# First projection of eight block pairs by seven half-size products

## The chip, the cores and the metric

The kernel runs on one core of a Trainium2 chip. The metric is the time of one execution on the device, in microseconds (us). The kernel before took 327.92 us (median of three runs, 327.44 to 328.18).

A core has five engines, each with its own queue of instructions that it works through in order: TensorE (PE; its weight loads are shown as PEld), VectorE (DVE), ScalarE (ACT), GpSimd (POOL) and SyncE (SP, which here only starts transfers). They wait for each other by semaphores. TensorE's products land in PSUM, which has eight banks of 128 partitions x 512 f32 values; VectorE and ScalarE read them from there.

## The reference

Sparse attention of 8 batches x 8 heads x 576 tokens x 64 values (four heads with a local mask, four with a strided one) gives x, 4608 tokens x 512. Then comes a bilinear feed-forward layer with d_ff = 1536:

```python
a = x @ w_a          # 4608 x 512 times 512 x 1536
b = x @ w_b
out = (a * b) @ w_out
```

The change touches only `a`, for some tokens and some features.

## The kernel before

**Tiles.** The 4608 tokens are nine tiles of 512 (`TTOK`, t = 0 to 8, `NT` = 9). x is held transposed in `xT`: 128 partitions x `KD` = 4 slices of the inner dimension x a ring of four batches of tokens. The 1536 features are `FD` = 12 blocks of 128. Two neighbouring blocks, 2g and 2g + 1, are pair g.

**First projection** (`ffn_ab`, `ab_mm`). For each tile and block, a takes four products of 128x128 weights with 512 tokens, one for each slice of the inner dimension, summed in one PSUM bank; b takes four more in another. ScalarE copies a to `a_sb` (L638), VectorE multiplies it by b from PSUM into `pf` (bf16, L641), in an order of tokens that suits the second projection.

**Second projection.** Tiles 2 to 8 (`FAST_Y`) take it by seven products instead of eight on halves of the tokens, of the inner dimension and of the output columns (`products`, `y_plan`, and `y_tail` for the last tile). It needs sums of parts of `pf` (`fast_s`, L655, on VectorE, into `ps`) and of the weights (`fast_w`, L174, once). In the last tile, `y_tail` uses narrow banks that each take several results in turn: ScalarE copies one out (L686) and the next group of products goes into the same bank.

**Banks.** From the second stage on PSUM is cut into `mm` (three banks, in turn), `tp` (one bank), `o` (two banks) and `st` (two banks). `mm_bank` hands out mm, mm, mm, tp in a cycle of four. `st` and `o` belong to the attention, which runs one batch ahead of the feed-forward tiles; its last steps (batch 7) lie in tile 6. A bank is handed on only when whoever reads it is done.

**Order.** The program is written in the order in which each engine gets its instructions (a manual schedule). The main loop runs over slots, 16 to a tile: twelve blocks of the first projection, four quarters of the second. After each slot it issues what is tied to it: attention steps (`take`), and the list `at` (loads, transposes, `fast_s`). Where a slot has such a list, GpSimd first copies one value of the slot's result to `pace` (L947), so that what it issues next does not come too early.

Of the kernel before, what the change touches and what calls it, by code (L numbers as in the profile page):

```python
# [7 lines left out]
F32 = mybir.dt.float32  # L8
BF16 = mybir.dt.bfloat16
I16 = mybir.dt.int16  # L10
ALU = mybir.AluOpType
# [13 lines left out]
VW = 128  # L25
WCH = (0, 2, 5, 9, 12)
FAST_Y = (2, 3, 4, 5, 6, 7, 8)


@with_exitstack  # L30
def kernel(
# [10 lines left out]
    nc = tc.nc  # L42
    B, H, S, D = q.shape
# [5 lines left out]
    KD = d_model // 128  # L49
    FD = d_ff // 128  # L50
    TTOK = 512
    NT = n_tok // TTOK
# [7 lines left out]
    fsb = ctx.enter_context(tc.tile_pool(name="ffn", bufs=2))  # L60
    pst = ctx.enter_context(tc.tile_pool(name="pst", bufs=1, space=bass.MemoryType.PSUM))
    dram = ctx.enter_context(tc.tile_pool(name="dram", bufs=2, space=bass.MemoryType.DRAM))

    psum4 = {}

    def open_psum(stack, **bufs):
        for nm, n in bufs.items():
# [8 lines left out]
    qz_pair = [(const.tile([128, 2, 2, S], BF16, name=f"qz{i}l"), const.tile([128, 2, 2, RS * GP], BF16, name=f"qz{i}s"))  # L76
               for i in range(2)]
    qz_buf = [[tuple(t[:, j] for t in pair) for j in range(2)] for pair in qz_pair]
    kT_buf = [(const.tile([128, 2, PAD + S], BF16, name=f"kT{i}l"), const.tile([128, 2, RS * GP + 48], BF16, name=f"kT{i}s"))
              for i in range(2)]  # L80
    vl_buf = [const.tile([128, HL * 6, VW], BF16, name=f"vl{i}") for i in range(2)]
# [76 lines left out]
    XR = 4  # L158
    xT = const.tile([128, KD, XR * S], BF16)
    wa_sb = wp.tile([128, KD, d_ff], BF16)  # L160
    wb_sb = wp.tile([128, KD, d_ff], BF16)
    wo_sb = wp.tile([128, FD, d_model], BF16)

    FG = FD // 2
    HT = TTOK // 2
# [437 lines left out]
    pfs = {}  # L603
# [3 lines left out]
    def mm_bank(shape):  # L607
        nm = "tp" if used[0] % 4 == 3 and used[0] >= 0 else "mm"
        used[0] += 1
        return psum4[nm].tile(shape, F32, tag=nm, name="mm")  # L610

    def ab_mm(t, f, ab, kks, mid=None, first=0, last=KD - 1, ws=(0, 1)):
        n = min(TTOK, XR * S - TTOK * t % (XR * S))
        cuts = [(0, n)] + ([(n, TTOK - n)] if n < TTOK else [])
        for w, ps_ in [((wa_sb, wb_sb)[i], ab[i]) for i in ws]:
            if mid and ps_ is ab[1]:
                mid()
            for kk in kks:
                for c0, n in cuts:
                    x0 = (TTOK * t + c0) % (XR * S)  # L620
                    nc.tensor.matmul(ps_[:, c0:c0 + n], lhsT=w[:, kk, 128 * f:128 * (f + 1)], rhs=xT[:, kk, x0:x0 + n],  # L621
                                     start=(kk == first and c0 == 0), stop=(kk == last and c0 == cuts[-1][0]))

    def ffn_ab(t, f, mid, ab=None):
        if f == 0:
            pfs[t] = fsb.tile([128, FD, TTOK], BF16, tag="pf", name="pf", bufs=1)
        pf = pfs[t]
        if ab is None:
            ab = [mm_bank([128, TTOK]) for _ in range(2)]
            if f == 0:  # L630

                late = 1 if t == 1 else 3
                ab_mm(t, f, ab, [kk for kk in range(KD) if kk != late], last=-1)
                ab_mm(t, f, ab, [late], first=-1, last=late)
            else:
                ab_mm(t, f, ab, range(KD), mid)
        a_sb = fsb.tile([128, TTOK], F32, tag="a_sb", name="a_sb")
        nc.scalar.copy(a_sb, ab[0])  # L638
        if t in FAST_Y:
            halves = lambda x: x.rearrange("p (a i s) -> p a i s", i=2, s=16)  # L640
            nc.vector.tensor_mul(pf[:, f, :].rearrange("p (i a s) -> p a i s", i=2, s=16), halves(a_sb), halves(ab[1]))  # L641
        else:
            nc.vector.tensor_mul(pf[:, f, :], a_sb, ab[1])  # L643
        return pf[:1, f, :1]

    pss = {}

    def fast_s(t, n, gs):
        if t not in pss:
            pss[t] = nat.tile([128, FG * 5 * SW], BF16, tag="shared", name="ps").rearrange("p (n g m) -> p n g m", g=FG, n=5)  # L650
        s = pss[t][:, :, gs, :HT]
        x = pfs[t].rearrange("p (g e) (i m) -> p e i g m", e=2, i=2)[:, :, :, gs]
        a, b, op = ((x[:, 0, 1], x[:, 1, 1], ALU.add), (s[:, 0], x[:, 0, 0], ALU.subtract),
                    (x[:, 0, 0], x[:, 0, 1], ALU.subtract), (x[:, 1, 0], s[:, 1], ALU.subtract))[n]
        nc.vector.tensor_tensor(s[:, n], a, b, op=op)  # L655

    yst = {}
# [144 lines left out]
    with tc.manual_schedule(engines={ENG.PE, ENG.SP, ENG.Pool, ENG.DVE, ENG.Activation}):  # L802
# [30 lines left out]
        for nm in ORDER:  # L833
            if nm[0] == "*":
                spin(int(nm[1:]))
            elif nm == "C0":
                for x, cp, n in ((raw[0], nc.vector.tensor_copy, "k"), (raw[1], nc.scalar.copy, "q")):
                    t = nats[0, n, False][:, 0:2].rearrange("p h r d -> p (h r d)")
# [21 lines left out]
            elif nm[0] == "F":  # L860
                f = int(nm[1])
# [6 lines left out]
                elif nm == "F0B":  # L868
                    first[f].append(psum4["o"].tile([128, 512], F32, tag="o", name="ab"))
                ab_mm(0, f, first[f], {"A": (0, 1), "B": (0, 1), "b": (2,), "c": (3,)}[nm[2]],  # L870
                      ws={"A": (0,), "B": (1,)}.get(nm[2], (0, 1)))
# [5 lines left out]
        for t in range(NT):  # L877
            slots += [(ffn_ab, t, f) for f in range(FD)] + [(ffn_ys if t in FAST_Y else ffn_y, t, j) for j in range(4)]
        for b in range(1, B):
# [9 lines left out]
        def do(i, fn, *args):  # L889
            at.setdefault(i, []).append(lambda: fn(*args))  # L890

        soon = {}
        for t in FAST_Y[:-1]:
            soon[16 * t + 10] = [lambda t=t: fast_s(t, 2, slice(4, 6))]
            soon[16 * t + 11] = [lambda t=t, n=n: fast_s(t, n, slice(4, 6)) for n in (0, 1)]
# [5 lines left out]
        for b in range(FIRST_D, B):  # L901
            g0 = 16 * (b - 2)
            if b == FIRST_D:
                do(0, load_qk, b, False)
                do(1, load_qk, b, True)
                do(16, load_vl, b)
                for h in range(HL):
                    do(20 + h, load_vs, b, (h,))
            else:
                for h in range(HL):  # L910
                    do(g0 + h + (2 if b == FIRST_D + 1 else -2), load_qk, b, False, (h,))
                    do(g0 + h + (6 if b == FIRST_D + 1 else 2), load_qk, b, True, (h,))
                    do(g0 + h + 10, load_vs, b, (h,))
                do(g0 + (10 if b == FIRST_D + 1 else 7), load_vl, b)
            gs = {2: (14, 14, 15, 15, 16, 16, 17, 17, 18, 18), 3: (8, 9, 10, 11, 12, 13, 14, 15, 16, 17)}.get(b) or (
                3, 5, 7, 9, 12, 13, 14, 15, 16, 17)
            for (z, nm, part), g in zip(((0, "k", 0), (0, "k", 1), (0, "q", 0), (0, "q", 1), (1, "k", 0), (1, "k", 1),
                                         (1, "k", 2), (1, "q", 0), (1, "q", 1), (1, "q", 2)), gs):
                if (b, z, nm, part) != (FIRST_D, 0, "k", 1):
                    do(g0 + g, step_D, b, z, nm, part)  # L920
        for h in range(HL):
            do((7, 7, 8, 9)[h], spread_vs, 1, h, nc.vector.tensor_copy)
        do(1, zero_qz, 1, nc.vector, ((1, 1),))
# [7 lines left out]
        for g in range(FG):  # L931
            for n in (2, 0, 1, 3):
                do(16 * (NT - 1) + 2 * g + 1, fast_s, NT - 1, n, slice(g, g + 1))
        for t in FAST_Y[:-1]:
            for slot, n, z0, z1 in ((4, 0, 0, 2), (5, 2, 0, 2), (6, 1, 0, 2), (7, 3, 0, 2), (8, 2, 2, 4), (9, 0, 2, 4),
# [45 lines left out]
```

## Time and profile before

| what | us |
| --- | --- |
| median of three runs | 327.92 |
| the profiled execution | 327.27 |
| its span, first to last instruction | 325.6 |
| first projection of tile 6 (with attention between) | 229.5 to 251.2 |
| first projection of tile 7 | 261.2 to 281.9 |
| first projection of tile 8 | 291.1 to 311.8 |
| second projection of tile 8, products | 311.8 to 321.2 |

The granted TensorE clock is 1.00 throughout. How to read the rows: a group's row has the line, engine, operation, output <- inputs with their shapes, the count, the busy time in us and the mean duration of one in ns, and then the time that the engine sat idle just before them with what ended it. A timeline row has start, length, engine, line and operation; an `xN` row is N such instructions in a row, in square brackets is the idle time before it. A chain row has start, length, and the engine and line of that piece. Matmuls are pipelined: one row lasts longer (379 ns for 512 columns, 273 for 256) than the step from one to the next, which is what a stream of them costs.

### The profile page before, as it was taken

How to read it: one execution, taken by the hardware profiler on the slowest of the kernel's cores; microseconds unless marked ns; L12 is line 12 of the kernel's file. 1: busy time of each engine (PE TensorE's matmuls, PEld its weight loads, DVE VectorE, ACT ScalarE, POOL GpSimd, SP SyncE). 2: the span in 40 equal slices, each digit the busy share in tenths (PEclk: the TensorE clock that was granted, in tenths of full speed). 3: DMA queues.
4: the chain of work that ended last, by engine and by line, in shares of the span. 5: the costliest groups of instructions: out<-in, count | busy, mean ns of one | idle time of the engine just before them, and what ended most of it. 6: DMA issues, size and time to landing. Idle time of an engine off the chain costs nothing.

```text
span 325.6 us, 7280 instructions
## 1 busy us (share of the span) xinstructions
PE 319.7 (98%) x2632; PEld 204.6 (63%) x2632; DVE 247.9 (76%) x530; ACT 183.6 (56%) x305; POOL 150.3 (46%) x279
## 2 busy tenths in 40 slices
PE   8999999999999999999999999999999999999994
PEld 7754565455555587557999885569555944674474
DVE  6766887888778899898889888988877645726652
ACT  6764775478764576457644765476547733323341
POOL 8936739599857554854476247633001001100000
PEclk9999999999999999999999999999999999999999
DMA  9999999899999989999999999899155040004004
GB/s 157 159 204 200 204 182 186 153 176 132 143 210 137 140 86 98 120 215 135 105 98 204 156 97 113 181 193 103 30 128 125 2 129 0 3 0 131 0 0 131
DMA packets 110723, 40.43 MB, mean 124 GB/s; under 512 B 88672, under 2 KB 107744, under 8 KB 110688
## 3 DMA queue, kind: packets, MB, share of 16 engines
q0 software_dynamic: 85968, 19.48, 65.5%
q1 hardware_dynamic: 24576, 20.42, 24.9%
q8 instruction: 21, 0.34, 0.5%
q14 instruction: 14, 0.11, 0.1%
q10 hardware_dynamic: 144, 0.07, 0.1%
HBM read 39.51 MB, written 10.91 MB: 155 GB/s over the span
## 4 chain that ended last, share of the span: by engine, by line
PE 94%; DMA 2%; DVE 1%; ACT 1%; issue 1%; POOL 0%; POOLq 0%
PE mm L621 54%; PE mm L709 17%; PE mm L773 6%; PE st L387 4%; PE o L465 2%; PE o L524 2%; DMA shared<-in_q_dram 2%; PE mm L738 2%; PE end L738 1%; PE ab L621 1%; PE misc L154 1%; PE tp L549 1%; PE tp L295 1%; PE st L400 0%; PE tp L286 0%
## 5 line engine op out<-in xcount | busy, mean ns | idle before, releaser
L621 PE MATMUL mm<-xT,wa_sb 128*128 128x512 bf16 (+1 forms) x472 | 110.3, 357 | 0.0
L621 PE MATMUL mm<-xT,wb_sb 128*128 128x512 bf16 (+1 forms) x472 | 110.2, 357 | 0.0
L638 ACT COPY a_sb<-mm 128x512 f32<-128x512 f32 x106 | 62.1, 586 | 71.3 <-PE mm L621 70.6
L641 DVE TENSOR_TENSOR pf<-a_sb,mm 128x512 bf16<-128x512 f32 x84 | 57.3, 682 | 26.6 <-PE mm L621 22.5
L947 POOL CAST pace<-pf 1x1 f32<-1x1 bf16 x87 | 23.7, 273 | 109.6 <-DVE pf L641 93.1
L621 PEld LDWEIGHTS <-wb_sb 128*128 128x128 bf16 x480 | 46.5, 98 | 44.0 <-issue 0.2
L621 PEld LDWEIGHTS <-wa_sb 128*128 128x128 bf16 x480 | 43.7, 98 | 31.3
L408 ACT ACTIVATE p<-st 72x576 bf16<-72x576 f32 (+1 forms) x56 | 36.4, 650 | 14.7 <-PE st L387 14.5
L540 DVE TENSOR_TENSOR xT<-o,xr 64x288 bf16<-64x288 f32 x48 | 21.4, 446 | 15.3 <-ACT xr L534 14.9
L709 PEld LDWEIGHTS <-ps 128*128 128x128 bf16 x288 | 28.0, 98 | 3.1
L686 ACT COPY y_sb<-mm 128x512 f32<-128x512 f32 (+1 forms) x28 | 15.6, 556 | 17.8 <-PE mm L709 14.5
L709 PE MATMUL mm<-wf,ps 128*128 128x256 bf16 x216 | 25.5, 273 | 0.0
L533 ACT ACTIVATE xr<-o 64x576 f32<-64x576 f32 x28 | 18.1, 648 | 11.9 <-PE o L524 11.6
L773 PE MATMUL mm<-wo_sb,pf 128*128 128x512 bf16 x96 | 23.4, 379 | 0.0
L242 POOL DMA_DIRECT2D vs<-in_v_dram x24 | 19.6, 820 | 4.9 <-PE mm L709 2.4
L709 PEld LDWEIGHTS <-pf 128*128 128x128 bf16 x216 | 20.2, 98 | 2.6 <-issue 0.2
L534 ACT ACTIVATE xr<-xr 64x576 f32<-64x576 f32 x28 | 19.1, 683 | 0.9
L709 PE MATMUL mm<-wo_sb,pf 128*128 128x256 bf16 x144 | 18.5, 273 | 0.1
L211 POOL DMA_DIRECT2D kl<-in_k_dram x24 | 16.0, 667 | 5.5 <-issue 2.9
L211 POOL DMA_DIRECT2D ql<-in_q_dram x24 | 16.2, 674 | 5.0 <-DMA wo_sb<-in_moe_w_out_dram 3.9
L643 DVE TENSOR_TENSOR pf<-a_sb,mm 128x512 bf16<-128x512 f32 x22 | 14.9, 675 | 4.5 <-ACT a_sb L638 3.0
L655 DVE TENSOR_TENSOR ps<-pf 128x512 bf16<-128x512 bf16 (+1 forms) x48 | 17.7, 379 | 0.4
(147 smaller groups left out, 452.9 us busy)
## 6 DMA issues: line engine op xcount, KB each, us to landing
out_dram<-y_sb SPq DMA_DIRECT2D x12, 512.0 KB, 4.8
out_dram<-y_sb SPq DMA_DIRECT2D x11, 256.0 KB, 3.1
vl<-in_v_dram POOLq DMA_DIRECT2D x6, 384.0 KB, 7.7
kl<-in_k_dram POOLq DMA_DIRECT2D x24, 72.0 KB, 3.1
ql<-in_q_dram POOLq DMA_DIRECT2D x24, 72.0 KB, 3.1
vs<-in_v_dram POOLq DMA_DIRECT2D x24, 72.0 KB, 4.2
wo_sb<-in_moe_w_out_dram POOLq DMA_DIRECT2D x4, 384.0 KB, 9.9
natk<-in_k_dram POOLq DMA_DIRECT2D x20, 72.0 KB, 3.4
```

Source lines behind the costliest of these rows:

```text
L211: nc.gpsimd.dma_start(out=t[32 * h:32 * h + 32], in_=src[b, h].rearrange("(i y) d -> y i d", y=32))
L242: nc.gpsimd.dma_start(out=vs_buf[b % 2][:, h, :, 0:D], in_=v[b, HL + h].rearrange("(p r) d -> p r d", r=RS))
L408: nc.scalar.activation(p_flat(p)[:M, :2 * W].rearrange("p (i n) -> p i n", n=2 * n), st[:M].rearrange("p a (i n) -> p (a i) n", n=256)[:, ...
L533: nc.scalar.activation(r, sums, ACT.Ln)
L534: nc.scalar.activation(r, r, ACT.Exp, scale=-1.0)
L540: nc.vector.tensor_mul(dst.rearrange("d (p r) -> d p r", r=RS)[:, :, G * half:G * (half + 1)], o[:64, j, :W].rearrange("d (g p) -> d p g", ...
L621: nc.tensor.matmul(ps_[:, c0:c0 + n], lhsT=w[:, kk, 128 * f:128 * (f + 1)], rhs=xT[:, kk, x0:x0 + n], start=(kk == first and c0 == 0), sto ...
L638: nc.scalar.copy(a_sb, ab[0])
L641: nc.vector.tensor_mul(pf[:, f, :].rearrange("p (i a s) -> p a i s", i=2, s=16), halves(a_sb), halves(ab[1]))
L709: nc.tensor.matmul(bank[b][:, q], lhsT=lhs(g, q), rhs=rhs(g), start=k in "172" and q == 0 and g == 0, stop=g == FG - 1, skip_group_check=True)
L773: nc.tensor.matmul(ybank[j], lhsT=pf[:, f, 128 * j:128 * (j + 1)], rhs=wo_sb[:, f], start=(f == 0), stop=(f == FD - 1))
L947: nc.gpsimd.tensor_copy(pace, done)
```

## The change

Eight pairs, g = 1 to 4 of tile 7 and g = 0 to 3 of tile 8 (`FAST_A`), take `a` of both blocks by seven products instead of eight. The 512 tokens are two halves (k), the inner dimension two halves of two slices each (j), the pair two blocks (e). Each product is two narrow matmuls of 256 columns (c = 0, 1). They need four sums of weight quarters, made once by VectorE in tile 6, and four sums of token quarters per tile. The sums are stored in tiles of the attention that are no longer used (`vl`, `qz`), as are the results of odd pairs (`kT`).

Products 1, 6, 5 and 3 add up in one bank X, in `st` for even g and in `o` for odd g. After each of them ScalarE copies the bank out, as one quarter of the result. Products 7 and 4 share a bank Z, product 2 has Y, and b of the two blocks takes one bank each; these four come from `mm` and `tp`. Product 7 goes by ScalarE to `p7`. VectorE adds Y to quarter (0,0) and Z to quarter (1,0); GpSimd adds `p7` to quarter (1,1). Then VectorE multiplies both blocks, block 2g + 1 first. The matmuls of b are put between the products of a. A pair takes two slots; the first ends behind product 2.

In tile 8, one of the four sums for the second projection (n = 2) of pairs 0 to 2 goes to GpSimd, one pair later. The diff, in its core:

```diff
+FAST_A = {7: (1, 2, 3, 4), 8: (0, 1, 2, 3)}
...
         pf = pfs[t]
+        if f // 2 in FAST_A.get(t, ()):
+            if f % 2 == 0:
+                pairs[t, f // 2] = a_pair(t, f // 2)
+            return next(pairs[t, f // 2])
...
+    wav = wa_sb.rearrange("p (j c) (g e m) -> p j c g e m", c=2, e=2, m=128)
+    wsum_a = [flat.rearrange("p (c g m) -> p c g m", c=2, g=FG)
+              for flat in [vl_buf[0].rearrange("p a b -> p (a b)")[:, 12 * 128 * z:12 * 128 * (z + 1)] for z in range(2)]
+              + [t.rearrange("p a b c -> p (a b c)")[:, :12 * 128] for t in qz_pair[0]]]
+    xsum = {t: qz_pair[1][t - 7].rearrange("p a b c -> p (a b c)")[:, :8 * HT].rearrange("p (n c m) -> p n c m", n=4, c=2)
+            for t in FAST_A}
+
+    def wsum_make(n):
+        w, s_ = (lambda e, j: wav[:, j, :, :, e]), wsum_a
+        a, b, op = ((w(1, 0), w(1, 1), ALU.add), (s_[0], w(0, 0), ALU.subtract), (w(0, 0), w(1, 0), ALU.subtract),
+                    (w(0, 1), s_[1], ALU.subtract))[n]
+        for c in range(2):
+            nc.vector.tensor_tensor(s_[n][:, c], a[:, c], b[:, c], op=op)
+
+    def x_part(t, j, k):
+        x0 = TTOK * t % (XR * S) + HT * k
+        return xT[:, 2 * j:2 * j + 2, x0:x0 + HT]
+
+    def xsum_make(t, n):
+        s_ = xsum[t]
+        a, b = ((x_part(t, 0, 1), x_part(t, 0, 0)), (x_part(t, 1, 1), s_[:, 0]), (x_part(t, 1, 1), x_part(t, 0, 1)),
+                (x_part(t, 1, 0), s_[:, 1]))[n]
+        nc.vector.tensor_tensor(s_[:, n], a, b, op=ALU.subtract)
...
+    def a_pair(t, g):
+        pf = pfs[t]
+        pool, nm = ((pst, "st"), (psum4["o"], "o"))[g % 2]
+        X = pool.tile([128, 2, 512], F32, tag=nm, name="ax")[:, 0, :HT]
+        a = ([fsb.tile([128, TTOK], F32, tag="a_sb", name="a_sb") for _ in range(2)] if g % 2 == 0 else
+             [t.rearrange("p h n -> p (h n)")[:, :2 * TTOK].bitcast(F32) for t in kT_buf[0]])
+        got = {k: psum4[nm].tile([128, TTOK], F32, tag=nm, name="mm")
+               for k, nm in zip((1, "Z", "Y", 0), (("mm", "mm", "tp", "mm"), ("tp", "mm", "mm", "mm"))[g % 2])}
+        Z, Y = got["Z"][:, :HT], got["Y"][:, :HT]
...
+        plan = {"1": (X, w(0, 0), x(0, 0)), "2": (Y, w(0, 1), x(1, 0)), "3": (X, ws(3), x(1, 1)), "4": (Z, w(1, 1), xs(3)),
+                "5": (X, ws(0), xs(0)), "6": (X, ws(1), xs(1)), "7": (Z, ws(2), xs(2))}
...
+        P("1")
+        nc.scalar.copy(quarter(0, 0), X)
+        b_mm(1, (0, 1, 2))
+        P("6")
+        nc.scalar.copy(quarter(1, 0), X)
+        b_mm(1, (3,))
+        P("7")
+        nc.scalar.copy(p7, Z)
+        P("2")
+        nc.vector.tensor_tensor(quarter(0, 0), Y, quarter(0, 0), op=ALU.add)
+        yield None
+        P("5")
+        nc.scalar.copy(quarter(1, 1), X)
+        nc.gpsimd.tensor_tensor(quarter(1, 1), quarter(1, 1), p7, op=ALU.add)
+        if (t, g - 1) in later:
+            later.pop((t, g - 1))()
+        b_mm(0, (0, 1))
+        P("4")
+        nc.vector.tensor_tensor(quarter(1, 0), Z, quarter(1, 0), op=ALU.add)
+        P("3")
+        nc.scalar.copy(quarter(0, 1), X)
+        b_mm(0, (2, 3))
+        mult(1)
+        mult(0)
+        yield pf[:1, 2 * g + 1, :1]
...
+        if (t, n) == (NT - 1, 2) and {gs.start, gs.start + 1} <= set(FAST_A[t]):
+            later[t, gs.start] = lambda: nc.gpsimd.tensor_tensor(s[:, n], a, b, op=op)
+            return
         nc.vector.tensor_tensor(s[:, n], a, b, op=op)
...
+        for n in range(4):
+            do(16 * (NT - 3) + 2 * n + 2, wsum_make, n)
+        do(16 * (NT - 2) - 1, xsum_make, NT - 2, 0)
+        for n in (2, 1, 3):
+            do(16 * (NT - 2), xsum_make, NT - 2, n)
+        for n in range(4):
+            do(16 * (NT - 2) + 12 + n, xsum_make, NT - 1, n)
```

Here `P(k)` issues the two matmuls of product k, `b_mm(e, kks)` those of b of block e for the slices kks, `mult(e)` the multiply of block e, and `quarter(e, k)` is the half k of block e's result.

More of the change, by code (lines that the diff above doesn't have):

```diff
@@ new lines, with P, b_mm, mult @@
+    pairs = {}
+    def a_pair(t, g):
[7 more added lines that the diff above has]
+        Z, Y = got["Z"][:, :HT], got["Y"][:, :HT]
+        p7 = fsb.tile([128, HT], F32, tag="p7", name="p7")
+        quarter = lambda e, k: a[e][:, HT * k:HT * (k + 1)]
+        w = lambda e, j: (lambda c: wav[:, j, c, g, e])
+        ws = lambda n: (lambda c: wsum_a[n][:, c, g])
+        x = lambda j, k: (lambda c: x_part(t, j, k)[:, c])
+        xs = lambda n: (lambda c: xsum[t][:, n, c])
+        plan = {"1": (X, w(0, 0), x(0, 0)), "2": (Y, w(0, 1), x(1, 0)), "3": (X, ws(3), x(1, 1)), "4": (Z, w(1, 1), xs(3)),
+                "5": (X, ws(0), xs(0)), "6": (X, ws(1), xs(1)), "7": (Z, ws(2), xs(2))}
+        def P(k):
+            bank, lhs, rhs = plan[k]
+            for c in range(2):
+                nc.tensor.matmul(bank, lhsT=lhs(c), rhs=rhs(c), start=k in "172" and c == 0, stop=c == 1, skip_group_check=True)
+        x0 = TTOK * t % (XR * S)
+        def b_mm(e, kks):
+            f = 2 * g + e
+            for kk in kks:
+                nc.tensor.matmul(got[e], lhsT=wb_sb[:, kk, 128 * f:128 * (f + 1)], rhs=xT[:, kk, x0:x0 + TTOK],
+                                 start=kk == 0, stop=kk == KD - 1)
+        def mult(e):
+            halves = lambda v_: v_.rearrange("p (a i s) -> p a i s", i=2, s=16)
+            nc.vector.tensor_mul(pf[:, 2 * g + e, :].rearrange("p (i a s) -> p a i s", i=2, s=16),
+                                 halves(a[e]), halves(got[e]))
+        P("1")
[23 more added lines that the diff above has]
+        yield pf[:1, 2 * g + 1, :1]
@@ L646 @@
+    later = {}
     pss = {}
```

## The prediction

> **What bounds the kernel now.** First the page's head and the table of who waited for whom, cut to TensorE:
>
> ```profile
> span 325.6 us, 7280 instructions
> PE 319.7 (98%) x2632; PEld 204.6 (63%) x2632; DVE 247.9 (76%) x530; ACT 183.6 (56%) x305; POOL 150.3 (46%) x279
> ...
> PE misc L154 <- PEq L965: 0.9, 1, 0.9
> PE o L465 <- DVE xr L491: 0.2, 1, 0.2
> PE tp L289 <- DMA shared<-in_q_dram: 0.2, 1, 0.2
> ```
>
> TensorE waits 1.3 us in all, and none of it in the last tiles. So the time is what TensorE has to stream, and a change pays what it takes off that stream minus the gaps that it opens. The chain that ended last, in order of time, prices the stream (start, length, what):
>
> ```profile
> 261.34 20.72 PE mm L621 x96
> 282.06 9.17 PE mm L709 x84
> 291.23 20.72 PE mm L621 x96
> ```
>
> The two L621 rows are the projections of tiles 7 and 8: 20.72 / 96 = 215.8 ns for a product of 512 columns. The L709 row gives 9.17 / 84 = 109.2 ns for one of 256, though its weights change each time. Switching between narrow and wide costs nothing there: the three rows touch.
>
> **What is taken off.** A pair of blocks takes 16 wide products now (8 for a, 8 for b). After, a takes 7 products x 2 halves of the inner dimension = 14 narrow ones, and b keeps 8 wide: 16 x 215.8 = 3453 ns against 14 x 109.2 + 8 x 215.8 = 3255 ns. That is 198 ns a pair and **1.58 us for eight pairs**. All of it lies on TensorE's stream.
>
> **What is added, and beside what.** Prices, from the groups by shape and from the first rows of the tail (L738), which has the same pattern as the pairs:
>
> ```profile
> L641 DVE TENSOR_TENSOR pf<-a_sb,mm 128x512 bf16<-128x512 f32 x12 | 8.3, 688 | 8.6 <-PE mm L621 5.9 <-ACT a_sb L638 2.7
> L684 DVE TENSOR_TENSOR y_sb<-y_sb 128x256 f32<-128x256 f32 x2 | 0.9, 426 | 1.2 <-ACT y_sb L686 1.2
> L688 DVE TENSOR_TENSOR y_sb<-mm,y_sb 128x256 f32<-128x256 f32 x1 | 0.4, 425 | 1.5 <-PE mm L738 1.5
> ...
> 311.79 0.82 PE L738 MATMUL mm<-wo_sb,pf 128*128 128x256 bf16 x6
> ...
> 312.44 1.50 PE L738 MATMUL mm<-wf,ps 128*128 128x256 bf16 x12
> ...
> 312.69 0.37 ACT L686 COPY y_sb<-mm 128x256 f32<-128x256 f32 x1 [0.98 <-PE mm L738]
> ...
> 315.74 0.82 PE L738 MATMUL end<-wf,ps 128*128 128x256 bf16 x6
> ...
> 315.94 0.37 ACT L686 COPY y_sb<-mm 128x256 f32<-128x256 f32 x1 [0.94 <-PE mm L738]
> ...
> 316.40 0.82 PE L738 MATMUL mm<-wo_sb,ps 128*128 128x256 bf16 x6
> ```
>
> I lay one pair on a clock that starts with its first product. TensorE: P1 to 0.22, three b products to 0.87, P6 to 1.08, b to 1.30, P7 to 1.52, P2 to 1.74, P5 to 1.96, two b to 2.39, P4 to 2.60, P3 to 2.82, two b to 3.26.
>
> *The chain bank.* P1, P6, P5 and P3 share one bank, and each but the first must wait until ScalarE has copied the bank out. Between them lie 647, 652 and 650 ns of other products. In the tail a copy starts 0.20 us after its group's last product (315.74 to 315.94) and takes 0.37; products resume in the bank at 316.40, exactly 6 x 109.2 = 655 ns later, so copy and release fit into 655 ns. The first copy started 0.25 us after its group (312.44 to 312.69), and the next group in that bank, the second six of the row from 312.44, began 0.03 us late: twelve products back to back span 11 x 0.109 + 0.27 = 1.47 us, the row has 1.50. Of four such hand-overs three showed no gap and one 0.03. A pair has 3, eight pairs 24. I take a quarter of 24 at 0.035, **0.21 us**, and keep 0 and 24 x 0.037 = 0.89 as ends (0.25 + 0.37 + 0.065 = 0.685 needed, 0.648 there).
>
> *GpSimd's add* (quarter (1,1)) has no like in the trace. It can start at 1.96 + 0.20 + 0.37 + 0.06 = 2.59. Nearest rows: VectorE's add of the same shape, 0.43 us (L684 above), and GpSimd's one-input pass over 96 columns:
>
> ```profile
> L94 POOL TENSOR_SCALAR_AFFINE_SELECT msl<-msl 128x96 f32<-128x96 f32 x2 | 0.6, 284 | 0.1
> ```
>
> In proportion that is 284 x 256 / 96 = 0.76 us, and 1.5 for two inputs at one after the other. I take 0.76, the row on the same engine, and keep 0.43 and 1.5. The Trainium skill (GPSIMD Engine Reference, 3.1 Elementwise — side-by-side cycle accounting) gives 4497 ns for an add of 2048 f32 elements, in proportion an estimate of 0.56 us for 256, by which the sum below stays as it is; no row here shows such an add.
>
> *VectorE.* Its adds fall at 1.94 and 2.80 (0.42 each); then the multiply for b1 must wait for GpSimd: 2.59 + 0.76 = 3.35 to 4.04; the other follows to about 4.7, then the sums for the second projection. In tile 8 a pair holds two adds, two multiplies and three sums of 0.29 (the fourth goes to GpSimd): 0.85 + 1.38 + 0.87 = 3.10 of 3.26 us, so VectorE is nearly full but keeps up. Who waits: b1's bank is wanted again 1.30 into the next pair where that is an odd one (clock 4.56), 1.52 where an even one (4.77), and after the last pair by block 10 or 8 one block's a later (3.26 + 0.86 = 4.12). With release at 4.04 + 0.06 = 4.10, nobody waits, the last by 0.02 only. b0's bank is wanted at 5.2, free at 4.8. After tile 8's last pair, block 8's a takes the bank of Z, which VectorE frees at 3.29 against 3.26: **0.04 us** once.
>
> *ScalarE* has five copies of 0.37 a pair, 1.86 of 3.26 us. One collides: tile 8 begins with a pair, just when ScalarE still copies the last y product of tile 7 (the whole 512 columns):
>
> ```profile
> 291.07 0.81 PE L621 MATMUL mm<-xT,wa_sb 128*128 128x512 bf16 x3
> 291.27 0.59 ACT L692 COPY y_sb<-mm 128x512 f32<-128x512 f32 x1 [2.03 <-PE mm L709]
> ```
>
> (The timeline's rows start 0.16 us ahead of the chain's pieces, the latency of a product.) The copy of P1 would be ready to start at 291.07 + 0.22 + 0.20 = 291.49. Copies follow each other after 0.49 at best (229.47 to 229.95 in the timeline), so it starts at 291.76, ends at 292.13, and P6, due at 291.94, starts at 292.20: **0.26 us**. In tile 7 the first pair comes after two ordinary blocks and nothing collides.
>
> *Weight sums*: four sums in two halves of 128x768 bf16, at L174's 0.55 us, 4.4 us on VectorE in tile 6 (blocks 2, 4, 6, 8). There VectorE was busy 17.23 of the 21.70 us between 229.5 and 251.2. I walked its queue with them in: the multiply of block 9 comes 0.67 us late, and at 248.85, where VectorE waits for ScalarE's reciprocal in both orders, the delay is gone. A multiply may be 1.9 us late before its bank is missed (its bank is wanted three groups of 0.86 later, less 0.69). Cost nothing; without that cover the 4.4 us would be late at tile 6's second projection.
>
> *Token sums*: eight of 128x512, 0.42 each. Four lie at the start of tile 7, done at about 265.4, 0.1 us ahead of P6 of its first pair; four in tile 7's second projection, where VectorE sits idle 2.9 us at one go. Nothing. The three sums moved to GpSimd are wanted only in the tail, over 6 us later.
>
> **The sum**: -1.58 + 0.21 + 0.04 + 0.26 = -1.07 us. The profiled execution took 327.27 us, 1.67 more than its span, and would take 326.2; its span would be 324.5. The median shown, 327.92, lies 0.65 above that execution; with the same 1.07 off it gives 326.85, say **326.9**. 0.2% is 0.66 us, about what a measurement of this kernel can tell from no change.
>
> **Rivals.**
>
> *The chain bank is too tight everywhere.* If every hand-over needs the 0.685 us of the tail's first, 0.89 us goes instead of 0.21: -0.39, 327.5. For it: 3 to 8 ns less cover than the tail has, and most copies in the pairs wait for a second engine. Against it: three of the four rows. Chance 0.20.
>
> *GpSimd's add is slow and VectorE stands behind it* (slower). Multiplies queue behind the add, and b1's bank goes with them. From 0.78 us on, the two exits (blocks 10 and 8 after the last pairs) stall; from 1.16, each step from an even pair to an odd one; from 1.37, the others. At 1.5: release at 2.59 + 1.5 + 0.75 = 4.84, that is 0.72 at each of two exits, 0.28 at the three steps from an even to an odd pair, 0.07 at the other three, 2.5 us in all: +1.4, **329.4**. It turns slower than before from about 1.25 us on. The Trainium skill (GPSIMD Engine Reference, 8. Key points) speaks for it: GpSimd shares its SBUF interfaces with VectorE and the two contend when VectorE reads two inputs there. In tile 7 one such sum runs from 2.36 to 2.78, across the add's start at 2.59; waiting for it would cost 0.2 at tile 7's exit. No row of this trace shows the two at once. Chance 0.16.
>
> *Seven products cost what eight did*: narrow products among wide ones, with weights from buffers newly summed, run at 123 ns instead of 109 (14 x 123 = 8 x 215.8), and only the gaps remain: +0.51, 328.4. Against it the touching rows above; tile 6's eight narrow attention products fit into 0.26 us between wide ones. Chance 0.06.
>
> **Numbers.** Forecast 0.58. Faster by over 0.2%: the forecast, 0.58. Within: the tight bank and the third, 0.26. Slower: GpSimd's, 0.16. The range reaches from no chain gap at all, -1.28, with 0.4 us for scatter like that of the runs before, 326.2, to an add of about 1.35 us, 328.5; beyond lies about 0.15.
>
> **What would show it.** The L621 rows of tiles 7 and 8 shrink to 64 and 32 wide products, with 14 narrow per pair at 109 ns; each pair spans 3.26 us from P1 to P1. Idle time of TensorE before the chain products, released by ScalarE, gives the first cost; before b1's successor or the exits, released by VectorE, the rival's. GpSimd's row for the add gives its price. Tile 8's first P6 should start 0.26 late. I am wrong if pairs span more than 3.4 us, if tile 6 shows a gap, or if the end moves by other than the pairs' sum.

## The result, and the profile after

The changed kernel takes **326.3 us** (median of nine runs, 326.04 to 327.55), the kernel before on the same chip 327.92 (nine runs, 326.73 to 329.26). The ratio is 0.9958, 95% interval 0.9937 to 0.9978: 1.4 us faster, between 0.7 and 2.1. Run again beside the experiments, the same kernel took 326.2 against 327.66, ratio 0.9965 (0.9945 to 0.9985). The forecast was 326.9, within 326.2 to 328.5, and faster; the median came out 0.1 above the lower end of that range.

The page's head and the table of who waited for whom, cut to TensorE, of the changed kernel:

```profile
span 324.6 us, 7425 instructions
PE 317.0 (98%) x2651; PEld 209.4 (65%) x2680; DVE 258.5 (80%) x559; ACT 188.9 (58%) x329; POOL 160.3 (49%) x289
```

```profile
PE misc L155 <- PEq L1071: 0.9, 1, 0.9
PE mm L622 <- DMA xT<-xd: 0.2, 1, 0.2
```

TensorE is still busy for 98% of the span, and the span is 324.6 us where 324.5 was forecast (how far that is luck is told below). VectorE is 10.6 us busier and GpSimd 10.0, and no wait of TensorE for either is in the table. Short losses do not show there: a row of a product outlasts the step to the next by 0.16 us, and neither of the two losses read below (0.24 and 0.04 us) is in the table. The chain has the second projection of tile 7 at its old price, 84 products in 9.18 us (start, length, what):

```profile
281.42 9.18 PE mm L808 x84
290.63 0.59 ACT y_sb L791
```

The last row shown is new: for a moment the end hangs on ScalarE's copy at tile 8's start, the collision of the prediction.

**A measure free of what lies ahead.** The profiles differ by over a microsecond in where tile 7 starts (the two of the changed kernel by 0.70), from what lies ahead of it. So the runs are compared from the start of tile 7's third block (or first pair) to the start of the last twelve narrow products of the tail, here in the kernel before and in the changed one:

```profile
264.63 1.03 PE L621 MATMUL mm<-xT,wa_sb 128*128 128x512 bf16 x4
...
320.33 0.83 PE L738 MATMUL mm<-wo_sb,pf 128*128 128x128 bf16 x12
```

```profile
264.78 0.38 PE L699 MATMUL ax<-xT,wa_sb 128*128 128x256 bf16 x2
...
319.18 0.83 PE L837 MATMUL mm<-wo_sb,pf 128*128 128x128 bf16 x12
```

| kernel | from | to | length | against the change |
| --- | --- | --- | --- | --- |
| before | 264.63 | 320.33 | 55.70 | +1.30 |
| the change | 264.78 | 319.18 | 54.40 | 0 |
| the change, again | 264.08 | 318.47 | 54.39 | -0.01 |
| sums alone, no pairs | 264.78 | 320.48 | 55.70 | +1.30 |
| tile 7's pairs alone | 264.67 | 319.57 | 54.90 | +0.50 |
| less cover for the chain bank | 265.22 | 321.16 | 55.94 | +1.54 |
| GpSimd's add twice | 264.32 | 321.07 | 56.75 | +2.35 |
| nothing on GpSimd | 264.05 | 319.14 | 55.09 | +0.69 |
| weight sums at once | 266.01 | 320.40 | 54.39 | -0.01 (and 1.24 ahead of it) |
| last copy on VectorE | 264.81 | 318.96 | 54.15 | -0.25 |
| a fifth pair | 264.99 | 318.90 | 53.91 | -0.49 |
| a fifth pair, no bank left out | 263.92 | 317.93 | 54.01 | -0.39 |

The change takes 1.30 us off this stretch. Each row is one profile; rows that should be equal (the change twice, before and the sums alone) agree to 0.01. Six of the kernels in the table were run only once; their whole times are given below, but they differ for reasons ahead of the stretch too, so these kernels are judged by the stretch.

The span shows 1.0, since in this execution tile 7 starts 0.15 later (after the wait for a transposed load in the table above, at the start of tile 6, which the second profile of the same kernel does not have) and the end, from the last twelve products on, takes 5.4 us in place of about 5.25. So the forecast of the span came out to 0.1 by luck: the stretch gained 0.23 more than forecast, and two delays that the change is not known to cause took that back. The second profile of the changed kernel has a span of 323.9.

**A pair in tile 7**, from the timeline of TensorE in the changed kernel (start, length, what):

```profile
271.29 0.38 PE L699 MATMUL ax<-xT,wa_sb 128*128 128x256 bf16 x2
...
272.16 0.38 PE L699 MATMUL ax<-qz1l,vl 128*128 128x256 bf16 x2
...
273.03 0.38 PE L699 MATMUL ax<-qz1l,vl 128*128 128x256 bf16 x2
...
273.90 0.38 PE L699 MATMUL ax<-xT,qz0s 128*128 128x256 bf16 x2
...
274.55 0.38 PE L699 MATMUL ax<-xT,wa_sb 128*128 128x256 bf16 x2
```

The rows `ax` are products 1, 6, 5, 3 and the next pair's 1. They start 0.87, 1.74, 2.61 and 3.26 us behind the first: the clock of the prediction with no gap in it. All four pairs of tile 7 span 3.25 to 3.26, so no hand-over of the chain bank costs anything there.

**Tile 8's first pair**, the timelines of TensorE and of ScalarE in the changed kernel:

```profile
290.43 0.38 PE L699 MATMUL ax<-xT,wa_sb 128*128 128x256 bf16 x2
...
291.54 0.38 PE L699 MATMUL ax<-qz1s,vl 128*128 128x256 bf16 x2
...
293.92 0.38 PE L699 MATMUL ax<-xT,wa_sb 128*128 128x256 bf16 x2
```

```profile
290.63 0.59 ACT L791 COPY y_sb<-mm 128x512 f32<-128x512 f32 x1 [2.03 <-PE mm L808]
291.11 0.38 ACT L715 COPY a_sb<-ax 128x256 f32<-128x256 f32 x1
```

Product 6 starts 1.11 after product 1 in place of 0.87: 0.24 us lost, and the pair spans 3.49. ScalarE's copy of product 1 could have started at 290.43 + 0.22 + 0.20 = 290.85 and starts at 291.11, behind the copy of 512 columns. The other three pairs of tile 8 span 3.25 to 3.26.

**Tile 8's exit**, TensorE and VectorE in the changed kernel:

```profile
303.69 1.03 PE L622 MATMUL mm<-xT,wa_sb 128*128 128x512 bf16 x4
304.58 1.04 PE L622 MATMUL mm<-xT,wb_sb 128*128 128x512 bf16 x4
```

```profile
303.84 0.69 DVE L711 TENSOR_TENSOR pf<-kT0s,mm 128x512 bf16<-128x512 f32 x1
```

Block 8's a starts as soon as the pair's last two b products, from 303.26 on, are through. Four wide products take 0.863, so b was due at 304.553. It starts at 304.58, once the multiply that ends at 304.53 has freed a bank, and the next row follows at 305.46, 0.88 later in place of 0.863. So about 0.04 us is lost here, but at b, not at a.

The sum closes: -1.58 + 0.24 + 0.04 = -1.30, which is what the stretch measures.

### The profile page after: what moved, and what is told of

It reads as the page before. It is cut to its first block, busy times and chain, and to the rows that moved or that the text cites. A ratio compares the mean times of both kernels' runs of the same rounds, so it can differ in the third digit from the quotient of the medians.

```text
span 324.6 us, 7425 instructions
## 1 busy us (share of the span) xinstructions
PE 317.0 (98%) x2651; PEld 209.4 (65%) x2680; DVE 258.5 (80%) x559; ACT 188.9 (58%) x329; POOL 160.3 (49%) x289
## 4 chain that ended last, share of the span: by engine, by line
PE 88%; DMA 6%; POOL 2%; ACT 1%; DVE 1%; issue 1%; POOLq 0%
PE mm L622 46%; PE mm L808 14%; PE mm L872 6%; PE st L388 4%; PE mm L706 4%; PE o L466 2%; PE ax L699 2%; DMA xd<-xl 2%; PE o L525 2%; DMA xT<-xd 2%; DMA vl<-in_v_dram 2%; PE mm L699 2%; PE mm L837 2%; POOL shared L197 1%; PE end L837 1%; PE ab L622 1%
## 5 line engine op out<-in xcount | busy, mean ns | idle before, releaser
L622 PE MATMUL mm<-xT,wb_sb 128*128 128x512 bf16 (+1 forms) x404 | 93.3, 354 | 0.4
L622 PE MATMUL mm<-xT,wa_sb 128*128 128x512 bf16 (+1 forms) x391 | 92.1, 353 | 1.0 <-DMA xT<-xd 0.2
L643 ACT COPY a_sb<-mm 128x512 f32<-128x512 f32 x90 | 52.7, 586 | 53.8 <-PE mm L622 51.8
L622 PEld LDWEIGHTS <-wb_sb 128*128 128x128 bf16 x416 | 40.2, 98 | 36.6 <-DVE pf L711 0.4
L1053 POOL CAST pace<-pf 1x1 f32<-1x1 bf16 x83 | 24.9, 300 | 71.2 <-DVE pf L646 51.6
L646 DVE TENSOR_TENSOR pf<-a_sb,mm 128x512 bf16<-128x512 f32 x68 | 46.2, 680 | 9.6 <-PE mm L622 8.1
L622 PEld LDWEIGHTS <-wa_sb 128*128 128x128 bf16 x416 | 37.5, 98 | 24.4 <-issue 0.5
L1053 POOL COPY pace<-y_sb 1x1 f32<-1x1 f32 x23 | 5.2, 226 | 33.1 <-DVE y_sb L783 19.8
L706 PE MATMUL mm<-xT,wb_sb 128*128 128x512 bf16 x60 | 18.3, 379 | 0.1
```

The costliest lines, as they stand in the source:

```text
L706: nc.tensor.matmul(got[e], lhsT=wb_sb[:, kk, 128 * f:128 * (f + 1)], rhs=xT[:, kk, x0:x0 + TTOK], start=kk == 0, stop=kk == KD - 1)
L1053: nc.gpsimd.tensor_copy(pace, done)
```

## The experiments

The theory: the time is TensorE's stream, 198 ns less for each pair, plus the gaps that banks open; the chain bank has just enough cover, GpSimd's add just enough time, and the sums of weights and tokens cost nothing. The rivals: another price of the hand-over or of the add, hidden by slack that the theory did not see; sums that do cost; seven products that save less than counted.

**Is the stream the gain, and are the sums free?** Two kernels leave pairs out. Pairs in neither tile, all sums still made:

```diff
-FAST_A = {7: (1, 2, 3, 4), 8: (0, 1, 2, 3)}
+FAST_A = {7: (), 8: ()}
```

> All weight and token sums are made, but no pair uses them: both tiles take the first projection as before. Theory (the sums cost nothing, VectorE's idle time takes them): 55.70 us on the same measure as the kernel before, no gap in tile 6. Rival (the sums cost something that the pairs' gain hid): more than 55.75, or a gap in tile 6.

Measured: 55.70 over the stretch, the kernel before's to the hundredth, and no gap in tile 6 (a single run took 327.82 us, one of before 327.34). The sums cost nothing.

```diff
-FAST_A = {7: (1, 2, 3, 4), 8: (0, 1, 2, 3)}
+FAST_A = {7: (1, 2, 3, 4), 8: ()}
```

> Pairs in tile 7 only; tile 8 takes its first projection as before, though its token sums are still made. Measured from the start of tile 7's third block to the tail's last group of products, so that what differs ahead of the change stays out: 55.70 us in the kernel before, 54.40 in the changed one. Theory (each pair takes 0.198 us off TensorE's stream, tile 7's four leave no gap, the 0.28 us of gaps belong to tile 8): 55.70 - 0.79 = 54.91, no gap of TensorE in tiles 7 and 8. Rival (the gaps in tile 8 come from what tile 7's pairs leave behind on VectorE and ScalarE): a gap at tile 8's start here too, 55.1 or more.

Measured: 54.90, so four pairs give 0.80 = 4 x 0.200, and TensorE has no gap in either tile (a single run took 326.56, one of before 327.34). With the line above, tile 7's four pairs give their full 198 ns each and tile 8's four give 0.50, 0.79 less 0.24 and 0.04. The rival that narrow products cost more among wide ones falls.

**What has the chain bank left?** One b product is moved from ahead of product 6 to behind it:

```diff
-        b_mm(1, (0, 1, 2))
+        b_mm(1, (0, 1))
         P("6")
         nc.scalar.copy(quarter(1, 0), X)
-        b_mm(1, (3,))
+        b_mm(1, (2, 3))
```

> Two instead of three of b's products stand between products 1 and 6 of each pair (the third moves behind 6). The cover of the first hand-over of the chain bank falls from 648 to 432 ns, that of the second rises from 652 to 868. Theory (a hand-over needs 0.20 us to the start of ScalarE's copy, 0.37 for the copy and about 0.06 to the next product, 0.63 in all, so the 648 ns just covered it): every pair has one gap of 0.20 us before product 6, pairs span 3.45 us instead of 3.26, tile 8's first one 0.45 behind instead of 0.24, in all +1.6 us over the changed kernel, span about 326.2. Rival (hand-overs had plenty of room, what was costly is not there): no gap, span as the changed kernel's, 324.6. Second rival (0.685 needed): gaps of 0.25, +2.0 us.

TensorE and ScalarE of this kernel:

```profile
268.67 0.38 PE L699 MATMUL ax<-xT,wa_sb 128*128 128x256 bf16 x2
...
269.51 0.38 PE L699 MATMUL ax<-qz1l,vl 128*128 128x256 bf16 x2
```

```profile
269.08 0.37 ACT L715 COPY a_sb<-ax 128x256 f32<-128x256 f32 x1 [0.28 <-PE ax L699]
```

Product 6 was due at 268.67 + 0.218 + 0.432 = 269.32 and starts at 269.51: 0.19 us of gap, again in every pair, and 0.46 in tile 8's first. So a hand-over needs 0.432 + 0.19 = **0.62 us** from the last product in the bank to the next: 0.20 to the copy's start, 0.37 for the copy, 0.05 to release. Over the eight pairs the stretch is 1.54 us longer than in the change and 0.24 longer than before, so with this one product moved the pairs lose more than they gain (a single run took 328.3, one of before 326.49). In the change the cover is 0.647 to 0.652, so a hand-over has some 25 ns left, and of the 24 none has a gap but the one at tile 8's start, where ScalarE is late.

**How much may GpSimd's add take?** It is made twice, first into a spare tile:

```diff
+        nc.gpsimd.tensor_tensor(fsb.tile([128, HT], F32, tag="twice", name="twice", bufs=1), quarter(1, 1), p7, op=ALU.add)
         nc.gpsimd.tensor_tensor(quarter(1, 1), quarter(1, 1), p7, op=ALU.add)
```

> GpSimd makes its add of quarter (1,1) twice in each pair, first into a spare tile that nobody reads, then as before. The add that counts then ends about 0.68 us later (two adds of 0.73 that follow each other after about 0.68). Theory (the add decides when VectorE multiplies and when b1's bank comes free; it is free now at 4.05 on the pair's clock, then at about 4.80): 0.7 us lost at each of the two exits (wanted at 4.12), 0.25 at each of the three steps from an even to an odd pair (4.56), up to 0.05 at the other three (4.77): +2.2 us over the changed kernel, span about 326.8, with gaps that VectorE's multiply ends. Rival (GpSimd's add stands beside other work and decides nothing): no new gap, span 324.6.

Measured: +2.35 us against the change, where 2.2 was expected (a single run took 328.2, one of before 326.49). But most of the gaps lie elsewhere. Tile 7's exit has none; four of the eight pairs have 0.06 to 0.27 ahead of product 2, five have 0.15 ahead of b of block 2g, one 0.25 ahead of its first b product, and tile 8's exit has 0.47 ahead of block 8's a and 0.27 ahead of its b. TensorE, then VectorE and GpSimd at that exit:

```profile
305.34 1.02 PE L622 MATMUL mm<-xT,wa_sb 128*128 128x512 bf16 x4 [0.31 <-DVE kT0l L723]
```

```profile
304.21 0.74 DVE L755 TENSOR_TENSOR ps<-pf,ps 128x256 bf16<-128x256 bf16 x1
304.88 0.41 DVE L723 TENSOR_TENSOR kT0l<-mm,kT0l 128x256 f32<-128x256 f32 x1
305.21 0.41 DVE L733 TENSOR_TENSOR kT0s<-mm,kT0s 128x256 f32<-128x256 f32 x1
```

```profile
304.08 0.73 POOL L727 TENSOR_TENSOR twice<-kT0s,p 128x256 f32<-128x256 f32 x1 [0.92 <-ACT kT0s L726]
```

Block 8's a waits for VectorE's add of **Y** (L723), done at 305.29, not for the add of Z (L733), done at 305.62. This shows two things. First, banks are not all taken by the position that I had counted; the gaps fit an order in which each new tile takes the bank that was given back longest ago: Z, b of 2g + 1, b of 2g after an even pair, Y, Z, b of 2g after an odd one. Second, the delay reaches VectorE not only through the multiply behind the add. VectorE's sum at 304.21 took 0.74, while the same shape takes 0.29. It started while GpSimd was adding. The same happens in tile 7; VectorE and GpSimd there:

```profile
273.79 0.98 DVE L755 TENSOR_TENSOR ps<-ps,pf 128x512 bf16<-128x512 bf16 x1
```

```profile
273.76 0.73 POOL L727 TENSOR_TENSOR twice<-kT0s,p 128x256 f32<-128x256 f32 x1 [0.92 <-ACT kT0s L726]
```

The sum of 512 columns (0.42 as a rule) took 0.98 and ended at 274.77, 0.28 after GpSimd's add (274.49). In this kernel four sums with both inputs in SBUF start 0.03 to 0.14 after such an add, and all four end only 0.15 or 0.28 after it. It goes the other way too: a sum that starts at 300.52, 0.03 ahead of the add, keeps its 0.29, and the add takes 0.85 in place of 0.73. VectorE's adds with one input in PSUM, as the one at 305.21 above, keep their time beside GpSimd's.

**What does GpSimd carry?** The add and the three sums go back to VectorE:

```diff
-        nc.gpsimd.tensor_tensor(quarter(1, 1), quarter(1, 1), p7, op=ALU.add)
+        nc.vector.tensor_tensor(quarter(1, 1), quarter(1, 1), p7, op=ALU.add)
...
-        if (t, n) == (NT - 1, 2) and {gs.start, gs.start + 1} <= set(FAST_A[t]):
+        if False and (t, n) == (NT - 1, 2) and {gs.start, gs.start + 1} <= set(FAST_A[t]):
```

> GpSimd's add of quarter (1,1) and the three sums that tile 8 gave it go to VectorE. Theory (VectorE is nearly full in the pairs of tile 8: a pair takes it about 3.07 us when it waits for nobody, of 3.26): 3.07 + 0.36 + 0.33 = 3.75 us a pair there, so from tile 8's second pair on TensorE falls behind by up to 0.5 us a pair, +1.0 to +1.6 us in tile 8; in tile 7, with two sums of 0.35 to a pair instead of three of 0.29, about 3.1 us, no new gap. Span about 325.9. Rival (GpSimd's part is a detour that makes VectorE wait; without it multiplies start earlier): no new gap, the wait of block 8's b for its bank goes, span 324.55 or less.

VectorE, the first add of two pairs in turn:

```profile
295.67 0.42 DVE L723 TENSOR_TENSOR kT0l<-mm,kT0l 128x256 f32<-128x256 f32 x1
...
299.17 0.42 DVE L723 TENSOR_TENSOR a_sb<-mm,a_sb 128x256 f32<-128x256 f32 x1
```

Measured: +0.69, all of it at tile 8's exit (0.19 ahead of block 8's a, 0.53 ahead of its b, where the change has 0.03 to 0.04); a single run took 326.41, one of before 326.49. The direction was right, the size too large. VectorE takes 3.50 us for a pair, not the 3.75 expected, nor the 3.78 to which the durations of its rows add up: instructions that do not depend on each other overlap (the three adds start 0.33 apart with 0.42 each). It falls 0.25 behind a pair, and the slack in the banks takes that in until the last pair.

**How much slack has tile 6?** All eight halves of the weight sums after one slot:

```diff
-            do(16 * (NT - 3) + 2 * n + 2, wsum_make, n)
+            do(16 * (NT - 3) + 8, wsum_make, n)
```

> The eight instructions of the weight sums stand together behind block 8 of tile 6 instead of two each behind blocks 2, 4, 6 and 8. Theory (they cost nothing because VectorE's idle time in tile 6 absorbs them a pair at a time; a multiply may be 1.9 us late): 8 x 0.47 = 3.8 us in one go; the multiply of block 9 starts at about 250.6 instead of 248.0, its bank is wanted at 250.2 and free at 251.3: a gap of about 1.2 us in tile 6 before block 11, span about 325.8. Rival (VectorE's queue has far more room): no gap in tile 6, span 324.6. Second rival (attention waits too): more than 2 us.

TensorE in tile 6:

```profile
249.15 1.03 PE L622 MATMUL mm<-xT,wa_sb 128*128 128x512 bf16 x4
251.25 1.02 PE L622 MATMUL mm<-xT,wb_sb 128*128 128x512 bf16 x4 [1.08 <-DVE pf L646]
```

Due at 249.15 + 0.86 = 250.01, b starts at 251.25: one gap of 1.24, released by the late multiply. The span is 325.8, as expected, and the rest is the change's own 54.39. So the cover counted for tile 6 is of the right size, and spread over four slots the sums stay inside it.

**Is the collision at tile 8's start what costs 0.24?** The last copy of tile 7's second projection goes to VectorE, and one token sum a slot earlier:

```diff
-            nc.scalar.copy(part(0, 1), bank)
+            (nc.vector.tensor_copy if last else nc.scalar.copy)(part(0, 1), bank)
...
-            do(16 * (NT - 2) + 12 + n, xsum_make, NT - 1, n)
+            do(16 * (NT - 2) + 12 + min(n, 2), xsum_make, NT - 1, n)
```

(`last` is true for tile 7 alone.)

> The copy of the last product of tile 7's second projection goes from ScalarE to VectorE, and the fourth token sum of tile 8 is made one slot earlier, ahead of it. Theory (tile 8's first product 6 comes 0.24 us late because ScalarE still copies that product when product 1 of the pair is done): that gap goes, tile 8's first pair spans 3.26, the span falls by 0.24 against the changed kernel, to about 324.35. Rival (the first pair is late for another reason, its operands new or its bank just taken over): the gap stays.

ScalarE at tile 8's start:

```profile
290.87 0.37 ACT L715 COPY a_sb<-ax 128x256 f32<-128x256 f32 x1 [2.25 <-PE ax L699]
```

The first pair starts at 290.45 here; the copy follows its product by 0.20, the pair spans 3.25, and the gap is gone: -0.25 over the stretch. In whole times, 326.17 us, ratio 0.9955 (0.9939 to 0.997), which can't be told from the change's own.

**A fifth pair in tile 8.** With the collision gone, one pair more; the edits of the run before stay in. After an even last pair the code's own turn of banks seemed to put block 10's a on the bank of b of block 9, so the first version leaves one position out:

```diff
-FAST_A = {7: (1, 2, 3, 4), 8: (0, 1, 2, 3)}
+FAST_A = {7: (1, 2, 3, 4), 8: (0, 1, 2, 3, 4)}
...
+        if (t, f) == (NT - 1, 10):
+            used[0] += 1
```

> As the run before, and a fifth pair, g = 4, in tile 8; one bank is skipped in the cycle before block 10, so that its a takes the bank of Y and its b that of the pair's first b, as in tile 7. Theory (a pair is worth 0.198 us as long as whoever comes next does not want its banks early): span 0.198 + 0.24 + 0.04 below the changed kernel's, about 324.15, 0.5% under the kernel before. Rival (VectorE, which the pairs fill, has not caught up when the tail needs its sums): the tail starts late or has gaps, and the fifth pair is lost, 324.35 or more.

Measured: five pairs of 3.25 to 3.26 in tile 8, no gap at the exit, -0.49 over the stretch; 325.74 us (twelve runs), ratio 0.994 (0.9919 to 0.996).

The same without the two lines that leave a bank out:

> The fifth pair without skipping a bank: block 10's a then takes the bank of the pair's first b, which VectorE frees only after GpSimd's add and its own multiply. Theory (free at 4.05 on the pair's clock, wanted at 3.26): a gap of about 0.8 us before block 10 that VectorE's multiply ends, 0.8 above the run before, span about 324.95. Rival (banks at the exits are of no matter): as the run before.

Measured: -0.39 over the stretch, 325.48 us (ten runs), ratio 0.9937 (0.9918 to 0.9956). The expected gap of 0.8 was 0.10. TensorE and VectorE:

```profile
305.93 1.02 PE L622 MATMUL mm<-xT,wa_sb 128*128 128x512 bf16 x4
```

```profile
305.45 0.42 DVE L732 TENSOR_TENSOR a_sb<-mm,a_sb 128x256 f32<-128x256 f32 x1
305.98 1.29 DVE L711 TENSOR_TENSOR pf<-a_sb,mm 128x512 bf16<-128x512 f32 x2
```

Block 10's a, due at 305.83, starts at 305.93, right behind VectorE's add of Z (ends 305.87) and before the multiplies have begun. So it is in Z's bank, and my map of the banks fell here a second time. Both versions with a fifth pair beat both kernels by their medians; which of the two is better the times do not tell, and their intervals overlap the change's own. The traces do tell 0.4 to 0.5 us less in the stretch.

## Why the prediction was right, and where it was not

Direction and mechanism were right, and the size nearly: -1.07 us forecast, -1.30 in the stretch. That the span shows -1.0 is in part luck, as told above. Of the terms of the sum, one was mis-sized (the chain bank) and one right for a wrong reason (block 8). The price that no row of before had stands in the groups by shape of the changed kernel, over its last three tiles:

```profile
L727 POOL TENSOR_TENSOR a_sb<-a_sb,p 128x256 f32<-128x256 f32 x4 | 2.9, 734 | 7.9 <-ACT a_sb L726 7.9
```

Point by point:

- **The stream, -1.58.** Right. Tile 7's pairs alone give 0.80 for four, and a product of two narrow matmuls takes 0.218, as in the second projection. Each of the two tiles keeps 64 wide products, 32 of them for b in the pairs; the "64 and 32" of the prediction is a slip that no term rests on. The rival "seven products cost what eight did" falls.
- **The chain bank, +0.21.** Mis-sized: it is 0. Need in the pairs is 0.62 (less cover for one hand-over), cover 0.647 to 0.652. I had weighed the one late row of the tail (0.03) as a quarter of all cases; the pairs show it never. About half of that 0.03 was not even a hand-over: in before, 15 ns of it lie ahead of the last product of the group in front (at 313.00), and only 12 at the bank. The rival that every hand-over needs 0.685 falls with it. That the bank was close to its limit was right: 0.19 in one place per pair, for one product less, undoes the gain.
- **The collision at tile 8, +0.26.** Right: 0.24, by the copy that was named, and gone when that copy is moved.
- **Block 8, +0.04.** The size was right by luck, the step wrong: "block 8's a takes the bank of Z". It takes Y's and loses nothing; its b waits for the multiply of block 7. There the prediction had 0.02 us to spare (free at 4.10, wanted at 4.12); the bank came free at about 4.15, and 0.03 to 0.04 was lost. The count of positions in the code does not decide alone who waits, as four traces show (GpSimd's add twice, nothing on GpSimd, the fifth pair without a bank left out, and the change itself). Likewise b1's bank was not wanted at 4.12 at tile 7's exit, where a doubled add leaves no gap, and the earliest demand after an even pair came at product 2, not at product 7. The total did not suffer, since the add was short enough for either map.
- **GpSimd's add, 0.76 us.** Right: 734 ns by the row above, though nothing in the record ties an add of two inputs to the one-input pass that the price was scaled from, so that it came so close is luck. The rival's mechanism is real: at two adds in a row (1.53 to 1.66 us together) the stretch is 2.35 longer than in the change and 1.05 longer than before, where the prediction put 1.4 for 1.5 us. (By its own clock the steps between pairs stall from 1.22 and 1.43 us on, not from 1.16 and 1.37; its sum at 1.5 us is right.) Of the rule that the prediction took from the Trainium skill (GPSIMD Engine Reference, 8. Key points), that GpSimd and VectorE contend in SBUF, these traces show a part: 0.98 in place of 0.42 and 0.74 in place of 0.29 for sums that start during the add. The 0.2 us that it was to cost at tile 7's exit did not come: in the change the sum starts ahead of the add (270.39 and 270.65), and both keep their times, 0.41 and 0.74. "No row of this trace shows the two at once" was a misreading, as told below the list.
- **Sums at no cost.** Right: the stretch of the kernel with sums alone is as long as before's, and piled up in one slot they cost 1.24 where 1.2 was expected, by the cover that the prediction named (the eight instructions take 3.8 us in a row, not 4.4).
- **VectorE nearly full.** Right in kind: with GpSimd's share it falls behind by 0.25 a pair. The sum of durations overstates it, since neighbours overlap by about 0.09.
- **What was to show me wrong.** "Pairs span more than 3.4 us" was too loose a test: the first pair of tile 8 spans 3.49 by the very collision that the sum held. Tile 6 shows no gap of VectorE's making, and the end of the stretch moved by the pairs' sum.

**VectorE and GpSimd at once, in the kernel before.** There GpSimd's copies of one value to `pace` run beside VectorE's sums. All copies from `pf` (shortest, median and longest in ns), then one sum and one copy in tile 8:

```profile
L947 POOL CAST pace<-pf x87: 174/178/615, 60.3 to 312.9; 1x1 f32<-1x1 bf16 x87
```

```profile
309.21 0.49 DVE L655 TENSOR_TENSOR ps<-pf 128x256 bf16<-128x256 bf16 x2
309.42 0.31 POOL L947 CAST pace<-pf 1x1 f32<-1x1 bf16 x1 [3.14 <-DVE pf L641]
```

Of all 107 copies to `pace`, 48 meet no VectorE instruction that has two inputs in SBUF, and take 0.17 to 0.18 us. 44 start while one is running: 40 of these take 0.24 to 0.62 and end 0.03 to 0.05 after such an instruction, and the other four meet only its last 0.11 us and keep 0.18. 15 start first: 13 keep 0.17 to 0.18, and two that start within 0.01 us of VectorE's take 0.50. So the trace before the change already shows which engine waits for the other: the one that starts second.

Open: why the end took about 0.15 us longer after the last products, which no experiment was aimed at. Over the twelve profiles this end takes 5.2 to 5.6 us; the longest belongs to the kernel without pairs (sums alone) and the shortest to kernels with them, so the pairs by themselves do not explain it. Open too is the order in which banks are handed on, which was read from who waited for whom in the four traces and not tried by itself; and why the tail's first copy started 0.25 after its group where the others took 0.20.

## What to carry to other kernels

When one engine streams without a gap, price a change by what it takes off the stream and by each bank's need against its cover; here a need that sat some 25 ns inside its cover cost nothing, and one product less in between cost 0.19 us every time. Look first at the places where two patterns of work meet: both losses here (0.24 and 0.04 us) were at the start and the end of a row of pairs, and moving one copy to another engine brought one of them back. Who waits for a bank is to be read from when the last reader ends and the next writer starts, not from counting positions in the code alone.

## What the runs showed of the hardware

Two things were not expected. When VectorE works on two inputs in SBUF and GpSimd on SBUF as well, the one that starts second waits for the other. A sum on VectorE that starts just behind GpSimd's add takes 0.98 us in place of 0.42, or 0.74 in place of 0.29. A copy of one value on GpSimd that starts during such a sum takes 0.24 to 0.62 in place of 0.18, and an add that starts 0.03 behind one takes 0.85 in place of 0.73. An add that starts 0.26 behind a sum of 0.41 still keeps its 0.74. And instructions of VectorE that do not depend on each other start 0.33 us apart though each is shown with 0.42, so that a queue whose durations add up to 3.78 us a pair ran in 3.50.
